# Small moves in a gated mix of an S4D convolution and segmented attention: prologue order, who issues the reciprocals' transfers, and when the first row maxima are taken

## The chip, the cores and the metric

The kernel runs on one core of a Trainium2 chip. Times are device microseconds of one launch. A core has a matrix engine (PE, with its weight loads shown as PEld), a vector engine (DVE), a scalar engine (ACT), GpSimd (POOL) and SyncE (SP). SP, ACT and POOL can issue DMA transfers; each of these engines works through its own instructions in order. Three timed runs of the kernel before gave 769.55, 772.67 and 773.4 us, so the time before is their median, 772.67 us.

## The reference, cut to what matters

Two branches read the same input `x` (2048 positions, 448 channels) and are mixed by a gate.

```python
g = sigmoid((x * gate_w).sum(-1))
# branch a: S4D. K is a 2048-long filter per channel, from 256 complex modes
dt = exp(log_dt); A = -exp(log_A_real) + 1j * A_imag
C = (C_real + 1j * C_imag) * dt
K = 2 * real(einsum("dn,dnl->dl", C, exp(A * dt * l)))
a = causal_convolution(x, K) + x * D_skip
# branch b: 16 heads of 28, 4 segments of 512 positions
q, k, v = x @ wq, x @ wk, x @ wv
for s in range(4):
    a_dot = softmax(q_s k_s^T * scale + causal_mask) @ v_s
    a_mem = phi(q_s) M / (phi(q_s) z + 1e-6)
    o_s = sigmoid(beta) * a_mem + (1 - sigmoid(beta)) * a_dot
    M += phi(k_s)^T v_s; z += sum(phi(k_s))
b = concat(o) @ wo
out = g * a + (1 - g) * b
```

## The kernel before, in words

The program has three parts that follow each other.

**The prologue** (`prepare_params`, the first 60 us). The parameters of 448 x 256 modes lie as 112 partitions x 1024. DVE and ACT turn them into decays, phases and amplitudes. The amplitude and the angle of C come from `mx` and `mn`, the larger and the smaller of |C_real| and |C_imag|: `f` is the reciprocal of `mx` (`v.reciprocal(f, mx)`), then `f * mn`, whose arctangent `g` ACT takes; cosine and sine of `g` come later. Phases go out in two quantities: `a` (a rounded number of turns from A_imag) and `d` (the angle of C, rounded). Each is split into three bf16 parts by `parts`: ACT copies the value to a bf16 tile `sp`, the value less that copy is formed for the next part, and the tile is sent to DRAM (`SP<-sp`, issued by ACT). Six such transfers leave; `load_phase` then reads them back as `lh<-SP` on SP's queue, and the main loop of the next part needs them. Decays take the same road through `SD`, with POOL subtracting and issuing. The amplitudes are transposed on PE and copied to `cab`. An identity matrix with its sign turned, `nid`, lets PE form a low part as x minus its rounded value (`rest` in `project`, with the results `wvl`). The weights `wv` arrive in four loads `winv` on SP's queue. ACT needs the tables of different functions in turn, each change being an `ACT_TABLE_LOAD`.

**The first part** (60 to 420 us). A loop over 56 half blocks makes the filter: PE forms exponents and turns (`ps_arg`), ACT takes exp and sine, DVE multiplies (`X`, `Y`), PE sums (`ps_k`). The projections to q, k and v, and the first step of the transform of x, are fed between by a planner with costs (`Feed`, `RATES`, `ITEMS`).

**The second part** (420 us to the end, `second_half`). After a transform of the filter in eight rounds come 16 units `i`, one for each segment and group of four heads, each of six rounds `r`. In a round PE makes scores for the unit's weights (`weigh`: `ps_w`, exponentiated by ACT to `PT`, masked by POOL's affine select) and scores for the row maxima of the unit after next (`maxima`: `ps_mx`, reduced by DVE to `mx`). When a unit's maxima are done, PE transposes them (`ps_m<-ident,mx`), ACT copies them with turned sign to `mn`, and POOL sends `mn` into a spare row of the unit's q tile (`qu<-mn`); the unit's weights cannot start before that lands. `values` multiplies `PT` with v (`ps_pv`). The convolution's frequency steps (`convolve`: `ps_c`, products `pr` on DVE, copies `ks` and `bs` on ACT) and the ends of segments (`seg_end`) are put between. `turn_over` issues matmuls on a constant tile `wz` whose result nobody reads. The order on each engine is the order in which the code calls its helpers, which pin it: line 1538 of the profile is the helper for matmuls, 1541 for transposes, 1492 the one that orders ACT and DVE, 1554 the one for SP's DMAs.

At the end of a segment, `norm` and `recall` each need reciprocals: the denominators are spread over 128 partitions (`dn`, `dm`), `inverse` takes the reciprocal on DVE, splits it into two parts `rs`, and sends each part to rows of `r8` (`r<-rs` in the profile, line 1138, issued by ACT; six pairs in all). PE spreads these rows over the heads (`ps_m<-r,sel`), and DVE scales by the result. The PSUM tiles for these spread rows, and for the outputs `po`, alternate between the tags `m` and `c` where both are free.

Of the kernel before, what the change touches and what calls it, by code (L numbers as in the profile page):

```python
# [16 lines left out]
AF = mybir.ActivationFunctionType  # L17
# [6 lines left out]
D = 448  # L24
# [156 lines left out]
def prepare_params(nc, k, pool, early, gp):  # L181
# [69 lines left out]
    k.chained = last["v"].ins  # L251
    ts(dtp, dt, 1.0 / TWO_PI, None, ALU.mult)
    ts(dt2, dt, 2.0, None, ALU.mult)
    v.reciprocal(f, mx)
    yield 4
    nc.gpsimd.tensor_tensor(la, la, wide(dt), ALU.mult)
    for _ in parts(k.SD, la, nc.gpsimd.tensor_tensor, k.pdma):
        pass
    tt(mn, b, c, ALU.min)
    tt(f, f, mn, ALU.mult)  # L260
    act(g, f, AF.Arctan)
    yield 4
# [10 lines left out]
    ts(ai, a, 32.0, None, ALU.mult)  # L273
    ts(e, ai, MAG, None, ALU.add)
    stt(ai, e, MAG, ai, ALU.subtract, ALU.subtract)
    tt(cr, d, cr, ALU.subtract)
    nc.scalar.activation(cr, cr, AF.Abs)
    stt(ai, a, 0.5, ai, ALU.mult, ALU.add)
    ts(ci, ci, 0.0, -2.0, ALU.is_lt, ALU.mult)
    ts(ci, ci, 1.0, None, ALU.add)  # L280
    yield 2
# [2 lines left out]
    tt(ci, ci, ai, ALU.add)  # L284
    ts(e, ci, MAG, None, ALU.add)
    stt(d, e, MAG, ci, ALU.subtract, ALU.subtract)
    pa, pd = parts(k.SP[:, :, 0], a, tt, k.adma), parts(k.SP[:, :, 1], d, tt, k.adma)
    for s in range(3):
        for x in (pa, pd):
            next(x)  # L290
        yield 1
    act(c, g, AF.Sin, bias=math.pi / 2, scale=-1.0)
    act(b, g, AF.Sin)
    yield "phases"
# [6 lines left out]
    for nt in range(2):  # L301
        pt = k.ps("m")
        for j in range(4):
            k.tr(
                pt[:, 112 * j : 112 * j + 112], mx[:, j, 128 * nt : 128 * nt + 128], k.ident[:112, :112]
            )
        v.tensor_copy(
            k.cab[:, nt].rearrange("n (p j) -> n j p", j=4), pt[:, :D].rearrange("n (j p) -> n j p", j=4)
        )


# [412 lines left out]
def project(nc, k, pp, early, filling):  # L724
# [12 lines left out]

    nid = early.tile([112, 112], F32R, name="nid")
    with k.issue_after(k.chained):
        v.tensor_scalar(nid, k.ident[:112, :112], -1.0, None, ALU.mult)  # L740

    def rest(lo, x, hi):

# [240 lines left out]
def attend(nc, k, ap):  # L984
# [142 lines left out]
    def inverse(x, rows, dst):  # L1127


        rc = ap.tile([128, 64], F32, tag="rc", name="rc", bufs=2)  # L1130
        rs = ap.tile([128, 2, 64], F32R, tag="rs", name="rs", bufs=2)
        v.reciprocal(rc, x)
        v.tensor_copy(rs[:, 0], rc)
        v.tensor_tensor(rs[:, 1], rc, rs[:, 0], ALU.subtract)
        yield
        for b in range(2):
            o = rows + 4 * b
            k.pin(k.adma(
                dst[o : o + 4].rearrange("o h (i f) -> o (h i) f", f=64).bitcast(F32),
                rs[:, b].bitcast(F32),  # L1140
            ))
# [4 lines left out]
    def recall(s):  # L1146

        dn = ap.tile([128, 64], F32, tag="dm", name="dm", bufs=1)
        k.ldma(dn, k.DM[s - 1].rearrange("j h (i f) -> (j h i) f", f=64))
        yield  # L1150
        am[s] = ap.tile([128, 4, SEG], F32, tag="am", name="am", bufs=1)
        k.ldma(am[s], k.AM[:, :, s - 1].rearrange("h p q -> p h q"))
        yield
        v.tensor_scalar(dn, dn, 1e-6, None, ALU.add)
        yield from inverse(dn, 32, r8)
        yield
        for hg in range(4):
            pb = k.ps("c")[:, 0] if s == 3 and hg % 2 else k.ps("m")
            k.mm(pb, k.sel[32:40], r8[32:40, hg], start=True, stop=True)
            v.scalar_tensor_tensor(am[s][:, hg], am[s][:, hg], k.gh[:, hg : hg + 1], pb, ALU.mult, ALU.mult)  # L1160
            yield

    def norm(s):

        pvs = pvss[s]
        dn = ap.tile([128, 64], F32, tag="dn", name="dn", bufs=1)
        k.pin(k.pdma(
            dn,
            pvs.rearrange("(j e) h q -> e j (h q)", e=32)[28].rearrange("j (i f) -> j i f", f=64),
        ))  # L1170
        yield
        yield from inverse(dn, 0, r8)
        yield
        for hg in range(4):
            o = pvs[:, hg]
            pb = k.ps("c")[:, 0] if s == 2 and hg % 2 else k.ps("m")
            k.mm(pb, k.sel[0:8], r8[0:8, hg], start=True, stop=True)
            v.scalar_tensor_tensor(o, o, k.omg[:, hg : hg + 1], pb, ALU.mult, ALU.mult)
            if s > 0:
                v.tensor_tensor(o, o, am[s][:, hg], ALU.add)  # L1180
            yield
# [41 lines left out]
    def seg_end(s):  # L1223
# [26 lines left out]
        for t in range(4):  # L1250
            if t < 3:
                next(memory)
            po = k.ps("c")[:, 0] if s == 2 and t % 2 else k.ps("m")
            out_mm(s, t, po[:, :D], range(2))
            half.append(s)
            yield "po"
            half.pop()
            out_mm(s, t, po[:, :D], range(2, 4))
            store(s, t, po[:, :D], xts[t])
            yield "po"  # L1260
# [52 lines left out]
def second_half(nc, k, ap, tp, fp, fin):  # L1313
# [82 lines left out]
    for i in range(16):  # L1396
# [5 lines left out]
        for r in range(6):  # L1402
# [4 lines left out]
            if r < 2:  # L1407
# [2 lines left out]
                if i + r == 0:  # L1410
                    turn_over(4)
                peak(behind)
            if i == 0 and r in (0, 2):
                turn_over(4 - r)
                peak(behind)
            k.spread = r in (1, 2)
# [16 lines left out]
            if (i, r) in DIVIDE:  # L1433
                if k.half:
                    step(ends[0])
                k.divide(DIVIDE[i, r])
            if 1 <= i <= 12:
                x = next(cv, "rest")
                if x == "more":
                    step(cv)  # L1440
                busy = busy or x != "rest"
# [334 lines left out]
```

## Time and the profile before

| what | value |
|---|---|
| timed runs | 769.55, 772.67, 773.4 us |
| the profiled execution, its own time | 768.64 us |
| its span | 766.6 us (2.0 us lie around it) |
| PE busy | 677.8 us (88%) |
| DVE busy | 560.4 us (73%) |
| ACT busy | 502.8 us (66%) |
| POOL busy | 160.0 us (21%) |
| mean granted PE clock | 0.982 |

The span runs from the first instruction to the last. A line of the timeline gives start, length, engine, source line, operation, output and input tile, shapes, a count, and in brackets the time that the engine sat idle just before and what released it. A line of the windows view gives for a stretch of time its length and the busy time of PE, PEld, DVE, ACT and POOL (with counts), then the granted PE clock, the mean share of the DMA engines and GB/s. The chain of waits follows the work that ended last back to its start.

### The profile page before, as it was taken

The numbers are of one execution on the slowest core, as the hardware profiler recorded it, in microseconds if no ns is written. First come the engines' busy times: TensorE is split into PE (matmuls) and PEld (weight loads), VectorE is DVE, ScalarE is ACT, GpSimd is POOL, SyncE is SP. The second block draws the span as 40 slices with busy tenths as digits, with TensorE's granted clock in tenths as the row PEclk, the third lists the DMA queues.
The fourth block names the chain that finished last, engine by engine and source line by source line (L and its number), as shares of the span: only waits on it lengthen the run. The fifth ranks groups of instructions, "written<-read, shape, count | busy, mean of one in ns | idle before, by whom it ended". The sixth has DMA issues, their size and how long they took to land.

```text
span 766.6 us, 19838 instructions
## 1 busy us (share of the span) xinstructions
PE 677.8 (88%) x8295; PEld 369.8 (48%) x8295; DVE 560.4 (73%) x758; ACT 502.8 (66%) x621; POOL 160.0 (21%) x196
## 2 busy tenths in 40 slices
PE   1685998899898999989999998989999889988997
PEld 1362565566554764556665443433343334434433
DVE  7989778878899878899788334656664775576585
ACT  4777679888999889989887533565634463452220
POOL 5404301110111011100120002242411241133110
PEclk9998999999999999999999999999899999999999
DMA  9427774333574335641455878999866977548597
GB/s 235 141 67 236 229 247 127 107 110 111 177 230 136 111 102 183 207 161 49 152 194 200 322 260 304 279 357 360 270 233 200 354 231 255 212 129 322 140 285 224
DMA packets 91490, 158.01 MB, mean 206 GB/s; under 512 B 22090, under 2 KB 59458, under 8 KB 91402
## 3 DMA queue, kind: packets, MB, share of 16 engines
q1 hardware_dynamic: 85722, 153.55, 60.8%
q10 hardware_dynamic: 4656, 2.23, 1.2%
q8 instruction: 65, 1.06, 0.6%
q0 software_dynamic: 1024, 0.98, 0.4%
q14 instruction: 23, 0.19, 0.1%
HBM read 88.51 MB, written 60.24 MB: 194 GB/s over the span
## 4 chain that ended last, share of the span: by engine, by line
PE 50%; ACT 18%; DVE 13%; DMA 11%; issue 5%; SPq 2%; POOL 1%; ACTq 0%; DVEq 0%; POOLq 0%
PE ps_m L1538 19%; PE ps_c L1538 9%; ACT cs L1492 5%; PE ps_w L1538 5%; PE ps_arg L1538 4%; PE ps_pv L1538 4%; PE ps_mx L1538 4%; PE ps_k L1538 3%; ACT EY L1492 2%; DVE mx L1492 2%; DVE pr L1492 2%; DMA WD<-wsp 2%; DMA rest<-TB 1%; DVE pvs L1492 1%; DMA w<-WD 1%
## 5 line engine op out<-in xcount | busy, mean ns | idle before, releaser
L1492 DVE TENSOR_REDUCE mx<-ps_mx 128x2 f32<-128x1024 f32 (+3 forms) x128 | 102.5, 822 | 92.9 <-PE ps_mx L1538 83.2
L1492 ACT ACTIVATE PT<-ps_w 128x1024 f32<-128x1024 f32 (+1 forms) x96 | 84.5, 880 | 112.7 <-PE ps_w L1538 104.9
L366 POOL TENSOR_TENSOR EX<-EX,cab 128x1024 f32<-128x1024 f32 x28 | 53.5, 1913 | 288.6 <-ACT EX L1492 266.3
L1492 ACT ACTIVATE cs<-ps_arg 128x1024 f32<-128x1024 f32 x97 | 94.5, 1023 | 3.5 <-DVE Y L414 2.4
L1538 PE MATMUL ps_w<-qu,ku 32*128 32x512 f32 (+3 forms) x768 | 88.1, 345 | 6.9 <-ACT PT L1492 5.1
L1538 PE MATMUL ps_m<-xh,w 112*128 112x512 f32 x256 | 91.6, 410 | 1.0 <-DMA w<-WD 1.0
L1538 PEld LDWEIGHTS ps_w<-qu,ku 32*128 32x128 f32 x768 | 58.1, 187 | 70.3 <-ACT PT L1492 33.2
L1099 POOL TENSOR_SCALAR_AFFINE_SELECT PT<-PT 128x256 f32<-128x256 f32 (+1 forms) x96 | 47.4, 494 | 211.4 <-ACT PT L1492 210.7
L409 DVE TENSOR_TENSOR X<-EX,cs 128x1024 f32<-128x1024 f32 x56 | 70.3, 1255 | 12.8 <-ACT cs L1492 11.8
L1538 PE MATMUL ps_k<-Y,X 128*32 128x64 f32 x3584 | 63.8, 225 | 14.1 <-DVE Y L414 14.1
L1538 PEld LDWEIGHTS ps_k<-Y,X 128*32 128x32 f32 x3584 | 54.5, 113 | 40.2 <-DVE Y L414 22.9
L413 DVE TENSOR_TENSOR Y<-EY,cs 128x1024 f32<-128x1024 f32 x56 | 69.2, 1236 | 0.0
L1492 ACT ACTIVATE cs<-cs 128x1024 f32<-128x1024 f32 x56 | 59.2, 1057 | 1.3
L1538 PEld LDWEIGHTS ps_m<-xh,w 112*128 112x128 f32 x256 | 48.1, 188 | 21.1 <-issue 8.4
L1492 ACT ACTIVATE EY<-ps_arg 128x1024 f32<-128x1024 f32 x52 | 51.1, 1036 | 4.3 <-PE ps_arg L1538 4.1
L1538 PE MATMUL ps_arg<-ct,lh 64*128 64x512 bf16 x224 | 45.9, 385 | 7.0 <-ACT EY L1492 4.7
L1538 PE MATMUL ps_m<-xl,w 112*128 112x512 f32 x128 | 50.3, 393 | 0.0
L1538 PEld LDWEIGHTS <-lh 64*128 64x128 bf16 x392 | 20.0, 94 | 59.3 <-issue 46.9
L1538 PE MATMUL ps_pv<-PT,V 128*32 128x128 f32 (+3 forms) x512 | 44.2, 443 | 0.0
L1538 PE MATMUL ps_mx<-ku,qu 32*128 32x512 f32 (+3 forms) x256 | 43.4, 371 | 0.0
L415 DVE SCALAR_TENSOR_TENSOR Y<-EY,cs 128x512 f32<-128x512 f32 x56 | 40.0, 715 | 3.8 <-ACT cs L1492 2.5
L1538 PE MATMUL ps_arg<-ce,lh 64*128 64x512 bf16 x168 | 33.1, 399 | 10.8 <-ACT EY L1492 6.6
(224 smaller groups left out, 1296.5 us busy)
## 6 DMA issues: line engine op xcount, KB each, us to landing
w<-WD SPq DMA_DIRECT2D x32, 448.0 KB
qu<-QD SPq DMA_DIRECT2D x16, 512.0 KB
ku<-KD SPq DMA_DIRECT2D x16, 512.0 KB
GU<-gs SPq DMA_DIRECT2D x32, 224.0 KB
GK<-gs SPq DMA_DIRECT2D x8, 896.0 KB
gk<-GK SPq DMA_DIRECT2D x16, 448.0 KB
gu<-GU SPq DMA_DIRECT2D x16, 448.0 KB
ks<-ks SPq DMA_DIRECT2D x32, 224.0 KB
```

The source lines that it names most:

```text
L366: nc.gpsimd.tensor_tensor(o, o, cab, ALU.mult)
L409: v.tensor_tensor(X, ex, t[:, :, 0], ALU.mult)
L413: v.tensor_tensor(Y[:, :, :, :32], lo, y[:, :, :, ::-1], ALU.mult)
L415: v.scalar_tensor_tensor(Y[:, 1, :, 32:], ey[:, :, 32:], -1.0, y[:, 1], ALU.mult, ALU.mult)
L1099: nc.gpsimd.affine_select(sl, sl, pat, ALU.is_ge, 0.0, base=0, channel_multiplier=-1)
L1492: x = op(*args, **kw)
L1538: tc.keep_in_program_order(nc.tensor.matmul(*args, **kw))
```

## The change

In the prologue, `mn` is formed ahead of the reciprocal; `nid` and the two copies to `cab` go from DVE to ACT; the last step of `ai` moves ahead of the step on `cr`; the first part of `a` is split and sent sooner, so that the three rounds of (a, d) become one round of `a` alone, two rounds with both and one with `d` alone. In the second part, the twelve transfers `r<-rs` are issued by POOL in place of ACT; the third piece of unit 1's maxima in unit 0 comes in round 1 instead of round 2, with three fillers ahead of it instead of two; four fillers are added in unit 12, round 5; and the alternation between `c` and `m` starts with `c` in three places.

```diff
@@ prepare_params
+    tt(mn, b, c, ALU.min)
     v.reciprocal(f, mx)
     yield 4
     nc.gpsimd.tensor_tensor(la, la, wide(dt), ALU.mult)
     for _ in parts(k.SD, la, nc.gpsimd.tensor_tensor, k.pdma):
         pass
-    tt(mn, b, c, ALU.min)
     tt(f, f, mn, ALU.mult)
...
     stt(ai, e, MAG, ai, ALU.subtract, ALU.subtract)
+    stt(ai, a, 0.5, ai, ALU.mult, ALU.add)
     tt(cr, d, cr, ALU.subtract)
     nc.scalar.activation(cr, cr, AF.Abs)
-    stt(ai, a, 0.5, ai, ALU.mult, ALU.add)
+    pa = parts(k.SP[:, :, 0], a, tt, k.adma)
+    next(pa)
     ts(ci, ci, 0.0, -2.0, ALU.is_lt, ALU.mult)
...
-    pa, pd = parts(k.SP[:, :, 0], a, tt, k.adma), parts(k.SP[:, :, 1], d, tt, k.adma)
-    for s in range(3):
-        for x in (pa, pd):
-            next(x)
-        yield 1
+    pd = parts(k.SP[:, :, 1], d, tt, k.adma)
+    next(pa)
+    next(pd)
+    yield 1
+    next(pa)
+    next(pd)
+    yield 1
+    next(pd)
+    yield 1
...
-        v.tensor_copy(
-            k.cab[:, nt].rearrange("n (p j) -> n j p", j=4), pt[:, :D].rearrange("n (j p) -> n j p", j=4)
+        act(
+            k.cab[:, nt].rearrange("n (p j) -> n j p", j=4), pt[:, :D].rearrange("n (j p) -> n j p", j=4), AF.Copy
         )
@@ project
-        v.tensor_scalar(nid, k.ident[:112, :112], -1.0, None, ALU.mult)
+        act(nid, k.ident[:112, :112], AF.Copy, scale=-1.0)
@@ inverse
-            k.pin(k.adma(
+            k.pin(k.pdma(
@@ recall
-            pb = k.ps("c")[:, 0] if s == 3 and hg % 2 else k.ps("m")
+            pb = k.ps("c")[:, 0] if s == 3 and hg % 2 == 0 else k.ps("m")
@@ norm
-            pb = k.ps("c")[:, 0] if s == 2 and hg % 2 else k.ps("m")
+            pb = k.ps("c")[:, 0] if s == 2 and hg % 2 == 0 else k.ps("m")
@@ seg_end
-            po = k.ps("c")[:, 0] if s == 2 and t % 2 else k.ps("m")
+            po = k.ps("c")[:, 0] if s == 2 and t % 2 == 0 else k.ps("m")
@@ second_half
-            if i == 0 and r in (0, 2):
+            if i == 0 and r < 2:
                 turn_over(4 - r)
                 peak(behind)
...
                 k.divide(DIVIDE[i, r])
+            if (i, r) == (12, 5):
+                turn_over(4)
```

The first place is ACT's order in the prologue, from the last copy of the low weights (`wvl`) to the parts of `d`. `EY` and `EX` are the first exponentials, `sp<-pin_a` and `sp<-pin_d` the bf16 copies of the phases, `pin_cr` the absolute value on which `d` depends. Before:

```order
L1513 ACTIVATE wvl<-ps_m 112x448
L277 ACTIVATE pin_cr<-pin_cr 112x1024
L1501 ACT_TABLE_LOAD
L1501 ACTIVATE EY<-ps_arg 128x1024 x2
L1501 ACTIVATE EX<-ps_arg 128x1024
L1501 ACTIVATE EY<-ps_arg 128x1024 x2
L1501 ACTIVATE EX<-ps_arg 128x1024
L1513 ACTIVATE sp<-pin_d 112x1024
L236 DMA SP<-sp 448x1x256
L1513 ACTIVATE sp<-pin_a 112x1024
```

And now:

```order
L1521 ACTIVATE wvl<-ps_m 112x448
L1509 ACT_TABLE_LOAD
L1509 ACTIVATE EY<-ps_arg 128x1024
L278 ACTIVATE pin_cr<-pin_cr 112x1024
L1509 ACTIVATE EY<-ps_arg 128x1024
L1521 ACTIVATE sp<-pin_a 112x1024
L1509 ACTIVATE EX<-ps_arg 128x1024
L236 DMA SP<-sp 448x1x256
L1509 ACTIVATE EY<-ps_arg 128x1024 x2
L1509 ACTIVATE EX<-ps_arg 128x1024
L1521 ACTIVATE sp<-pin_d 112x1024
```

The copy of `a`'s second part and its DMA moved up between the exponentials, and `pin_cr` moved down behind the table load and the first exponential.

The second place is POOL at the start of the units: the sends of `mn` for units 0 and 1, between the masks of unit 0. Before:

```order
L990 MEMSET wo 128x1792
L1062 DMA qu<-mn 4x4x128
L1099 AFFINE_SELECT PT<-PT 128x2x128 x3
L1062 DMA qu<-mn 4x4x128
L1099 AFFINE_SELECT PT<-PT 128x2x128
L1099 AFFINE_SELECT PT<-PT 128x2x256 x2
```

And now:

```order
L996 MEMSET wo 128x1792
L1068 DMA qu<-mn 4x4x128
L1105 AFFINE_SELECT PT<-PT 128x2x128 x2
L1068 DMA qu<-mn 4x4x128
L1105 AFFINE_SELECT PT<-PT 128x2x128 x2
L1105 AFFINE_SELECT PT<-PT 128x2x256 x2
```

Unit 1's send now stands behind two masks in place of three, so one round sooner.

The third place is the third pair of reciprocal transfers, at the end of segment 1 (unit 8). Before, on ACT, they stand between two exponentials of `PT`:

```order
L1492 ACTIVATE ks<-ps_c 128x896
L1492 ACTIVATE PT<-ps_w 128x2x256
L1492 ACTIVATE PT<-ps_w 128x2x512
L1138 DMA r_5457<-rs 4x32x64 x2
L1492 ACTIVATE PT<-ps_w 128x2x512
L1492 ACTIVATE mn<-ps_m 16x128
L1492 ACTIVATE xt<-xt,gt 128x448 x2
```

Now they stand on POOL, between masks, behind the send that gathers the denominators (`dn<-pvs`):

```order
L1173 DMA dn<-pvs 128x1x64
L1105 AFFINE_SELECT PT<-PT 128x2x128
L1105 AFFINE_SELECT PT<-PT 128x2x256 x2
L1144 DMA r_5457<-rs 4x32x64 x2
L1105 AFFINE_SELECT PT<-PT 128x2x128 x2
L1068 DMA qu<-mn 4x4x128
L1200 TENSOR_TENSOR xt<-xt,dbc 128x448 x2
```

ACT's exponential no longer stands behind the pair; two of POOL's masks and the next unit's `qu<-mn` do.

## The prediction

> **What bounds the kernel now.** I read the page's chain of waits first, then the windows of the second part, then the idle times before PE's instructions.
>
> ```profile
> span 766.6 us, 19838 instructions
> PE 50%; ACT 18%; DVE 13%; DMA 11%; issue 5%; SPq 2%; POOL 1%; ACTq 0%; DVEq 0%; POOLq 0%
> 500.00:640.00 140.00, 129.24 (x1572) 55.51 (x1565) 88.12 (x117) 72.28 (x99) 42.83 (x70) 0.98 0.84 288
> 640.00:767.00 127.00, 114.23 (x944) 49.58 (x942) 81.08 (x113) 39.27 (x53) 24.20 (x42) 0.98 0.67 216
> ```
>
> In the second part PE is busy 129.24 of 140 us, that is 92%; POOL is busy 31% there. So a stop of PE there is lost time, and POOL has room. What one stop costs is more than its length, as the windows of 3.41 us along the granted clock show:
>
> ```profile
> 472.69:476.10 3.41, 1.79 (x25) 0.71 (x24) 1.14 (x2) 0.90 (x2) 0.64 (x1) 1.00 0.86 292
> 476.10:479.52 3.42, 3.42 (x28) 1.20 (x24) 0.40 (x1) 1.33 (x2) 0.41 (x1) 0.50 0.11 40
> 540.95:544.37 3.42, 2.39 (x37) 1.45 (x37) 3.42 (x6) 2.81 (x5) 3.42 (x5) 1.00 0.94 324
> 544.37:547.78 3.41, 3.41 (x33) 1.49 (x29) 0.92 (x3) 1.48 (x2) 0.65 (x3) 0.50 0.28 69
> 547.78:551.19 3.41, 3.41 (x33) 1.08 (x25) 1.69 (x3) 1.46 (x2) 0.99 (x2) 0.50 0.71 260
> 612.63:616.05 3.42, 2.03 (x36) 1.12 (x39) 1.26 (x2) 2.13 (x4) 0.92 (x2) 1.00 0.96 362
> 677.49:680.90 3.41, 1.95 (x25) 0.85 (x20) 3.41 (x6) 1.19 (x2) 1.27 (x2) 1.00 0.39 144
> 680.90:684.31 3.41, 3.32 (x22) 0.92 (x24) 2.17 (x6) 0.00 (x0) 0.00 (x0) 0.50 0.00 0
> ```
>
> Behind a window with PE busy 1.79, 2.39 or 1.95 us the clock is 0.50 for one or two windows, in which PE is busy throughout and the others wait; behind one with 2.03 it stays at 1.00, so the limit is not sharp. A window at half clock does 1.71 us of PE's work, which at full clock and 92% takes 1.85 us: an estimate of 1.56 us lost for each, and four of them stand in the second part.
>
> The Trainium skill (TensorE: Matmul & The Clock Gate, "What's actually happening") has the clock halve after an idle window of about 3.4 us; the length agrees with these windows, the condition does not, since PE was busy 1.79 to 2.39 us in those ahead of the drops.
>
> **The prologue: the front hides behind a load.**
>
> ```profile
> 19.03 2.51 DVE L214 TENSOR_TENSOR pin_mn<-pin_b,pin_c 112x1024 f32<-112x1024 f32 x1
> 23.25 1.21 DVE L214 TENSOR_TENSOR pin_f<-pin_f,pin_mn 112x1024 f32<-112x1024 f32 x1
> 25.91 1.06 ACT L214 ACTIVATE pin_g<-pin_f 112x1024 f32<-112x1024 f32 x1
> 20.62 2.69 SPq L1624 DMA_DIRECT2D gb<-in_B_beta  x4
> 23.40 0.37 SPq L756 DMA_DIRECT2D winv<-in_B_wv  x1
> 27.60 0.58 ACT L1513 ACTIVATE wvh<-winv 112x448 fp32r<-112x448 f32 x1 [0.64 <-DMA winv<-in_B_wv]
> ```
>
> With `nid` gone and `mn` ahead, DVE has `f` up to 3 us sooner (`mn` costs 2.51 here, 1.21 like the next product where it runs alone). Yet ACT's arctangent stands behind other work, and all that follows it behind `wvh` at 27.60, which waits for the fourth `winv`. SP issued that at 23.40, having been busy with `gb` until 23.31. A sooner DVE brings it at most 0.1 us. I take 0. `nid` on ACT lies in idle time ahead of the first weights.
>
> **The prologue: the tail.**
>
> ```profile
> 37.20 0.54 ACT L1513 ACTIVATE wvl<-ps_m 112x448 fp32r<-112x448 f32 x1 [1.02 <-PE ps_m L1538]
> 37.64 1.05 ACT L277 ACTIVATE pin_cr<-pin_cr 112x1024 f32<-112x1024 f32 x1
> 39.99 1.94 ACT L1501 ACTIVATE EY<-ps_arg 128x1024 f32<-128x1024 f32 x2
> 45.43 1.10 ACT L1513 ACTIVATE sp<-pin_d 112x1024 bf16<-112x1024 f32 x1
> 52.39 0.70 ACTq L236 DMA_DIRECT2D SP<-sp  x1
> 57.36 1.28 ACT L1494 ACT_TABLE_LOAD   x1
> 57.85 1.75 DVE L214 COPY cab<-ps_m 128x448 f32<-128x448 f32 x2 [0.32 <-PE ps_m L1541]
> 60.69 1.02 ACT L1494 ACTIVATE cs<-ps_arg 128x1024 f32<-128x1024 f32 x1 [2.04 <-DVE cs L386]
> ```
>
> ACT leaves 37.7 as before. Until the first copy of `d` it does the same table load, `pin_cr` and six exponentials, and in addition one copy of `a` (about 1.05): that copy starts near 46.5, not 45.43. From there one copy and one DMA fewer stand in the tail, but its steps follow each other: copy (1.1), subtract (1.2), copy, subtract, copy is 5.7 us, and `a`'s third copy with a DMA issue of 0.6 stands between the first two. The last `SP<-sp` leaves near 52.6, against 52.39: +0.2. Bounds: +1.1, when the whole extra copy stays, and -1.6, one copy and its issue saved. PE's value matmuls also begin an exponential later, which meets the same end. `cab` on ACT (two of about 0.6) comes ahead of its table load and fills idle time that was 2.04, while DVE is free sooner: +0.1, between -0.4 and +0.6. **The prologue: +0.3.**
>
> **The first maxima.**
>
> ```profile
> 464.73 1.02 ACT L1492 ACTIVATE PT<-ps_w 128x1024 f32<-128x1024 f32 x1 [3.80 <-PE ps_w L1538]
> 466.93 1.02 ACT L1492 ACTIVATE PT<-ps_w 128x1024 f32<-128x1024 f32 x1 [1.17 <-PE ps_w L1538]
> 468.69 0.61 POOL L1062 DMA_DIRECT2D qu<-mn  x1 [0.27 <-POOL PT L1099]
> 472.26 0.61 PE L1538 MATMUL ps_pv<-wz 128*128 128x512 bf16 x2
> 474.49 0.50 PE L1538 MATMUL ps_w<-qu,ku 32*128 32x512 f32 x2 [1.62 <-DMA qu<-mn]
> ```
>
> PE waits 1.62 us for unit 1's `mn`. A round here is 2.2 us (464.73 to 466.93), and the send moves up by one: that covers the wait. Late next is ACT's last exponential of unit 0, which frees the scores' tile: I leave 0.4 for it, an estimate, so 1.2 is won. Net one filler more is issued, some 0.2 us by the row of two. And the clock window at 476.10 should stay whole: -1.56. **-2.6**, between 0 and -3.2.
>
> **The reciprocals' transfers.**
>
> ```profile
> 536.03 7.01 DMA r<-rs
> 543.18 0.47 PE L1538 MATMUL ps_m<-r,sel 8*128 8x512 f32 x1 [0.70 <-DMA r<-rs]
> DMA to landing us min/median/max: 3.5/6.1/6.5
> 611.84 2.04 ACTq L1138 DMA_DIRECT2D r<-rs  x2
> 613.92 1.02 ACT L1492 ACTIVATE PT<-ps_w 128x1024 f32<-128x1024 f32 x1 [4.43 <-DVE mx L1492]
> 615.00 0.45 PE L1538 MATMUL ps_w<-qu,ku 32*128 32x384 f32 x2 [1.39 <-ACT PT L1492]
> 686.72 1.23 ACT L1492 ACTIVATE xt<-xt,gt 128x448 f32<-128x448 f32 x2 [0.41 <-DMA r<-rs]
> ```
>
> From ACT the first pair's second part lands 7.01 us after its issue, and PE waits 0.70 us. POOL has no row of its own for this transfer; the nearest is `dn<-pvs`, of the same 32 KB in pieces of the same 256 bytes, which lands after 3.5 to 6.5 us, 6.1 in the middle. Issued at 536.03 it lands at 542.1, ahead of PE's 542.48. So the wait goes (-0.7) and the two windows at half clock behind it (-3.1): **-3.8**, between 0 and -4.
>
> In the third pair ACT's exponential at 613.92 starts only when the two issues end (611.84 and 2.04 make 613.88), and PE waits 1.39 us for it. On POOL that block is gone: **-1.4**, between -0.5 and -1.8. In the fifth ACT waits 0.41 for the issue, and PE behind it: **-0.4**. At the other three no PE wait ends on ACT or on the transfer: 0. What now queues behind a waiting pair are POOL's masks and the next `qu<-mn`; the masks serve `values` a unit later, and POOL idles more than half the time, which hides two issues of 0.6.
>
> **The fillers of unit 12 and the tags.**
>
> ```profile
> 680.99 3.26 PE L1538 MATMUL ps_c<-pr,cb 64*64 64x448 f32 x16 [1.50 <-DVE pr L1492]
> 710.76 0.28 PE L1541 MATMUL ps_m<-ident,mx 128*16 128x128 f32 x1 [0.83 <-DVE tb L1492]
> ```
>
> Four fillers (about 1.0 us) go where PE waits 1.50 for `pr`: they cost nothing while that wait stands, and up to 1.0 if it is gone. They lift the window at 677.49 from 1.95 to some 2.8 us, above every row that fell: **-1.6**, between +1.0 and -1.6. With the tags exchanged the transpose at 710.76 no longer shares its tile with the output just before it, whose sum `tb` it awaits: **-0.8**; other pairs meet instead, so +0.8 is the other bound.
>
> **Sum**: 0.3 - 2.6 - 3.8 - 1.4 - 0.4 - 1.6 - 0.8 = -10.3. On the profiled execution's own 768.64 us (766.6 and 2.0 around) that is 758.3. The runs' median, 772.67, lies 4.0 above that execution; on it the sum gives 762.4, and I predict **762**.
>
> **The rivals.**
>
> The half-clock windows are not bought. For: three windows with 1.79, 1.95 and 2.03 busy had two fates, and one with 2.39 fell; a stop elsewhere may fall instead. Against: each drop here follows a window with a stop that goes. Then the waits alone are won: -1.0 - 0.7 - 1.4 - 0.4 - 0.8 + 0.3 = -4.0, or 768.7. The skill's clock page points the same way, by its idle window: stops of 1 to 2 us would not decide the clock.
>
> Other waits take over everywhere: the DMA engines' share is 0.84 from 500 to 640 us and 0.94 in the window at 540.95, so a PE that is sooner may meet loads that are not, and 5 us won early could be handed back. Against: beside `qu<-mn` and `r<-rs`, PE's idle rows longer than 0.3 us there name ACT and DVE, and no load of q, k or the convolution. About -0.5: 772.
>
> The front's 3 us come through after all, since SP and PE end almost together ahead of `winv`: -3 more, 759.4. The rows of `gb` speak against it.
>
> **Slower**: POOL's sends land late. They stand behind masks that wait for ACT, and a landing that is 3 us later than ACT's 7.0 makes PE wait 3 us more at each of the three norms: +9, with a half-clock window at each +4.7, against -6.5 from the rest: +7.2, or 780. It decides from a landing of about 9.2 us on (three times 2.2 eats 6.5). Against: no `dn<-pvs` took over 6.5. The skill (SBUF — State Buffer, "A bandwidth-pool intuition that's wrong") speaks for it: GpSimd cannot write its descriptors while DVE holds the port they share, and 620 ns become 3100. By that the landing of 6.1 would be an estimated 8.6 and the sum near -2. The rows here show no such lateness.
>
> **How the numbers follow.** Forecast 0.52 (756 to 766), the front comes through 0.06, clock not bought 0.22, taken over 0.12, slower 0.08. The range must leave out no more than two in ten: 756 to 770 leaves out the slower case, half of the taken-over one and a small tail below. A measurement tells this kernel from no change at about 0.5%, 3.9 us, so faster means below 768.8: 0.52 and 0.06, with 0.13 of the clock case, which lies on that line: 0.71. Within: 0.21. Slower: 0.08.
>
> **What would show it.** Right: the first `cs` of the loop near 61 us; no `qu<-mn` wait ahead of unit 1; no `r<-rs` wait; ACT's exponential in unit 8 directly behind its scores; clock 1.00 after unit 0, in segment 0's end and in unit 12. Wrong: a first `cs` that moves by more than 1 us, new drops of the clock in the second part, `r<-rs` from POOL landing after more than 7 us, or PE waiting for loads.

## The result, and the profile after

| kernel | timed runs, median | ratio to the kernel before, 95% interval |
|---|---|---|
| before, beside the changed one | 771.13 us (4 runs) | |
| changed | 761.99 us (760.22 to 762.35, 4 runs) | 0.9875 [0.9839, 0.9910] |
| changed, a second time | 761.63 us (759.63 to 763.95, 10 runs) | 0.9913 [0.9882, 0.9945] |

The change makes the kernel 0.9 to 1.3% faster; 762 us was forecast. Some executions run 5 to 40 us longer than the others of their kernel, the longest of them at a lower mean clock; they are left out of every ratio and mean here.

The page and the windows view of the changed kernel answer to the first rows of the prediction: PE's share of the chain rose from 50 to 55%, the transfers' fell from 11 to 5%, and between 500 and 640 us the granted clock is 1.00 (0.98 before).

```profile
span 760.4 us, 19830 instructions
PE 55%; ACT 18%; DVE 13%; issue 5%; DMA 5%; SPq 2%; POOL 1%; DVEq 0%; ACTq 0%; POOLq 0%
500.00:640.00 140.00, 130.22 (x1596) 56.52 (x1596) 92.45 (x124) 73.59 (x100) 49.37 (x80) 1.00 0.86 291
640.00:761.00 121.00, 110.25 (x895) 47.90 (x896) 75.77 (x103) 37.45 (x50) 25.52 (x44) 0.97 0.68 220
```

To see where the time went, the program is cut at eight instructions that both kernels have: A the first `cs` of the loop, B the end of the filter, C the first product with v (in unit 1), D a product with `pr` in unit 4, E the first output product of segment 0, F a product with `pr` in unit 10, G the first output product of segment 2, H the first `bt`. In the timeline of the kernel before, B to H are these rows (A, at 60.69, stands in the prediction):

```profile
421.27 1.77 PE L1538 MATMUL ps_w<-kb,s1k 32*128 32x448 f32 x8 [0.30 <-DVE kb L436]
475.38 1.28 PE L1538 MATMUL ps_pv<-PT,V 128*32 128x512 f32 x8
531.12 0.98 PE L1538 MATMUL ps_c<-pr,cb 64*64 64x448 f32 x8 [0.47 <-DVE pr L1492]
556.00 1.40 PE L1538 MATMUL ps_m<-wo,pvs 128*128 128x448 f32 x3
627.51 1.74 PE L1538 MATMUL ps_c<-pr,cb 64*64 64x448 f32 x16 [1.19 <-DVE pr L1492]
696.72 1.77 PE L1538 MATMUL ps_m<-wo,pvs 128*128 128x448 f32 x4 [0.89 <-DVE pvs L1492]
720.48 1.72 PE L1538 MATMUL ps_c<-bt,fc 128*64 128x448 f32 x8
```

And A to H in the timeline of the changed one:

```profile
62.35 1.02 ACT L1502 ACTIVATE cs<-ps_arg 128x1024 f32<-128x1024 f32 x1
422.65 1.77 PE L1546 MATMUL ps_w<-kb,s1k 32*128 32x448 f32 x8 [0.30 <-DVE kb L442]
475.50 1.06 PE L1546 MATMUL ps_pv<-PT,V 128*32 128x512 f32 x8
529.67 0.98 PE L1546 MATMUL ps_c<-pr,cb 64*64 64x448 f32 x8 [0.46 <-DVE pr L1500]
551.37 1.77 PE L1546 MATMUL ps_m<-wo,pvs 128*128 128x448 f32 x4
621.41 1.74 PE L1546 MATMUL ps_c<-pr,cb 64*64 64x448 f32 x16 [1.19 <-DVE pr L1500]
688.56 1.86 PE L1546 MATMUL ps_c<-wo,pvs 128*128 128x448 f32 x2 [0.88 <-DVE pvs L1500]
713.27 2.51 PE L1546 MATMUL ps_c<-bt,fc 128*64 128x448 f32 x6
```

The differences of such starts, in us, for these two and for the experiments below, as far as their profiles are used (the last column runs to the end of the span):

| kernel | to A | A-B | B-C | C-D | D-E | E-F | F-G | G-H | H-end |
|---|---|---|---|---|---|---|---|---|---|
| before | 60.69 | 360.58 | 54.11 | 55.74 | 24.88 | 71.51 | 69.21 | 23.76 | 46.12 |
| changed | 62.35 | 360.30 | 52.85 | 54.17 | 21.70 | 70.04 | 67.15 | 24.71 | 47.13 |
| after_again | 62.67 | 357.39 | 52.92 | 54.18 | 21.68 | 70.05 | 67.14 | 24.31 | 47.56 |
| maxima_old | 60.75 | 359.50 | 53.66 | 54.15 | 21.81 | 70.01 | 67.14 | 24.75 | 48.73 |
| prologue_old | 60.65 | 361.49 | 52.85 | 54.16 | 22.57 | 70.05 | 67.13 | 25.26 | 47.04 |
| unit12_old | 61.39 | 360.52 | 52.88 | 54.18 | 21.71 | 70.07 | 68.78 | 26.63 | 47.34 |
| recip_pool_alone | 60.72 | 360.48 | 54.18 | 54.16 | 21.70 | 70.10 | 69.35 | 26.39 | 46.42 |
| fillers_alone | 61.01 | 357.65 | 53.72 | 54.19 | 22.61 | 71.47 | 67.60 | 26.41 | 59.34 |
| fillers_two | 60.30 | 361.28 | 54.02 | 54.16 | 23.74 | 73.81 | 69.10 | 23.75 | 48.24 |
| fillers_three | 58.90 | 360.89 | 53.72 | 54.17 | 29.99 | 72.47 | 67.58 | 25.58 | 48.60 |
| cab_dve | 61.54 | 360.57 | 52.87 | 54.18 | 21.70 | 70.04 | 67.15 | 24.33 | 47.62 |
| fill_13 | 59.86 | 360.69 | 52.88 | 54.17 | 21.70 | 70.06 | 67.14 | 22.75 | 45.95 |
| fill_first | 60.79 | 357.52 | 53.32 | 54.21 | 22.02 | 73.75 | 67.13 | 23.15 | 47.91 |

Where nothing differs, a stage repeats within 0.1 us (54.15 to 54.21 in C-D, without the drop that stood there before); so what differs can be read. Between the two kernels five stages of the second part win 1.26, 1.57, 3.18, 1.47 and 2.06 us, and the last two give back 0.95 and 1.01. These last hold something new: a drop, that is a window at half clock, at two places that had none. Stretches of 3.41 us in the changed kernel, first at the three places whose drops went, then at the two where drops came (all but the first two lie on the edges of the clock's own windows):

```profile
476.10:479.50 3.40, 3.40 (x45) 1.18 (x41) 1.76 (x2) 2.49 (x4) 0.41 (x1) 1.00 0.84 217
544.40:547.80 3.40, 3.01 (x49) 1.18 (x41) 1.75 (x4) 1.46 (x3) 1.27 (x2) 1.00 0.92 299
674.82:678.23 3.41, 3.33 (x40) 1.20 (x40) 3.04 (x7) 1.49 (x2) 1.15 (x2) 1.00 0.02 5
685.06:688.47 3.41, 1.51 (x18) 0.69 (x17) 3.38 (x6) 0.66 (x2) 1.47 (x3) 1.00 1.03 418
688.47:691.88 3.41, 3.32 (x8) 1.21 (x10) 2.67 (x5) 0.00 (x0) 0.00 (x0) 0.50 1.03 409
708.95:712.36 3.41, 3.20 (x32) 1.78 (x23) 2.67 (x4) 2.08 (x3) 0.80 (x2) 1.00 0.41 128
712.36:715.78 3.42, 3.42 (x15) 1.45 (x14) 0.08 (x1) 0.60 (x1) 0.64 (x1) 0.50 1.04 253
```

The two stops between 685 and 688.5 us (0.96 us for `mx`, 0.88 for `pvs`) stood in the kernel before too, 1.00 and 0.89 us that ended at 694.68 and 696.72. There a window ended at 694.55, just ahead of the first stop's end, and shared the two out:

```profile
691.14:694.55 3.41, 2.53 (x32) 1.41 (x32) 3.28 (x5) 1.42 (x2) 2.91 (x4) 1.00 1.02 414
694.55:697.97 3.42, 2.27 (x19) 1.19 (x18) 3.35 (x7) 0.60 (x1) 0.64 (x1) 1.00 1.03 407
```

Now one window holds both, PE works 1.51 us in it, and the next runs at half clock. At the second place, 708.95, there is hardly a stop: PE works 3.20 us of 3.41. What is special about that window is said in the last section.

### The profile page after: what moved, and what is told of

Same layout as the page of the kernel before. It is cut to its first block, busy times and chain, and to the rows that moved or that the text cites. A ratio compares the mean times of both kernels' runs of the same rounds, so it can differ in the third digit from the quotient of the medians.

```text
span 760.4 us, 19830 instructions
## 1 busy us (share of the span) xinstructions
PE 673.1 (89%) x8284; PEld 368.6 (48%) x8300; DVE 556.8 (73%) x755; ACT 504.7 (66%) x624; POOL 167.2 (22%) x208
## 3 DMA queue, kind: packets, MB, share of 16 engines
q10 hardware_dynamic: 3072, 1.84, 0.9%
q0 software_dynamic: 1600, 1.39, 0.8%
q8 instruction: 65, 1.06, 0.6%
## 4 chain that ended last, share of the span: by engine, by line
PE 55%; ACT 18%; DVE 13%; issue 5%; DMA 5%; SPq 2%; POOL 1%; DVEq 0%; ACTq 0%; POOLq 0%
PE ps_m L1546 20%; PE ps_c L1546 10%; PE ps_w L1546 6%; ACT cs L1500 6%; PE ps_pv L1546 5%; PE ps_mx L1546 4%; PE ps_arg L1546 4%; PE ps_k L1546 4%; ACT EY L1500 2%; DVE pr L1500 2%; DVE mx L1500 2%; DMA WD<-wsp 2%; DVE pvs L1500 2%; DMA ce<-in_c_ce 1%; ACT L1500 1%
```

## The experiments

Twelve runs were made in three groups, each group on one chip and beside its own runs of the kernel before. Differences are between means of the runs, with standard errors. A drop is a stretch of one or more windows at half clock.

### Without the reciprocals' transfers on POOL (recip_on_act)

```diff
-            k.pin(k.pdma(
+            k.pin(k.adma(
```

> The changed kernel itself, timed in the same call as the three below so that they can be compared with it. Expected 0.9875 of the kernel before, so near 762 us where before takes 771.5. In its profile the half-clock windows are what matters: if they hang on stops of PE that are part of the program, the two of the second part come again at the end of unit 12 and in unit 14 (near 688 and 712 us); if they hang on how the free-running windows of 3.41 us happen to lie, at least one of them is gone or stands elsewhere.

> The changed kernel with the transfers of the reciprocals issued by ACT again. Theory (the sum of the prediction): -3.8 - 1.4 - 0.4 = -5.6 comes back, so 5.6 us above the changed kernel, with the wait for the first pair, the block of 1.4 us in unit 8 and one or two half-clock windows behind the first pair in the profile. Rival (clock windows were not bought by this): only the waits, 0.7 + 1.4 + 0.4 = 2.5 us come back. A second rival (POOL's later sends cost something elsewhere): below 1 us.

The changed kernel came to 761.84 ± 0.41 us, this one to 766.54 ± 0.61 (ratio 0.9983 [0.9951, 1.0015]): 4.7 ± 0.7 us come back, near the 5.6 of the theory and over the 2.5 of the waits alone. Of this kernel only the times are used, so where they come back isn't shown. In the changed kernel's second profile both drops of the second part stand at the same program places (686.6 and 710.5 us), and both of the first part are gone: so in these two executions the former repeat and the latter don't.

### The reciprocals' transfers on POOL alone (recip_pool_alone)

```diff
@@ the kernel before, inverse
-            k.pin(k.adma(
+            k.pin(k.pdma(
```

> The kernel before with the transfers of the reciprocals issued by POOL, and nothing else changed. Theory: 5.6 us faster than the kernel before, about 766, no PE wait for r in segment 0's end and clock 1.00 there. Rival without the clock: 2.5 us faster. Rival (it helps only together with the rest, since the end is reached through other waits): under 1 us.

764.80 ± 0.73 against 769.81 ± 0.80 us, 0.9933 [0.9901, 0.9965]: 5.0 ± 1.1 us faster. The stages D-E and E-F are those of the changed kernel to 0.06 us. F-G is not: without the fillers of unit 12 two windows at half clock stand there.

This kernel takes the first maxima as before, and PE waits for unit 1's send as before (1.50 us, where it was 1.62). Yet no drop follows:

```profile
474.48 0.50 PE L1538 MATMUL ps_w<-qu,ku 32*128 32x512 f32 x2 [1.50 <-DMA qu<-mn]
472.48:475.89 3.41, 1.91 (x26) 0.72 (x25) 1.24 (x2) 1.00 (x2) 0.64 (x1) 1.00 0.79 255
475.89:479.30 3.41, 3.41 (x45) 1.11 (x41) 1.83 (x2) 2.49 (x4) 0.41 (x1) 1.00 0.59 193
```

The window holds 1.91 us of PE's work, against 1.79 in the kernel before, and C-D is 54.16 without the sooner maxima. So the drop behind unit 0 is not tied to the wait alone.

### Without the sooner maxima (maxima_old)

```diff
-            if i == 0 and r < 2:
+            if i == 0 and r in (0, 2):
```

> The changed kernel with the third piece of unit 1's maxima in round 2 again. Theory: the wait for the send of unit 1 returns (1.0 net) with its half-clock window (1.56), so 2.6 us above the changed kernel. Rival without the clock: 1.0 us. If other waits had taken over: 0.

764.84 ± 0.59, so 3.0 ± 0.7 us slower than the changed kernel. But its profile splits this otherwise than the theory: B-C costs 0.81 more (53.66 against 52.85), and no drop follows in C-D, though PE waits 1.17 us for the send again: the window with that wait, at 471.58, holds 2.25 us of work. The rest lies in the finish, H-end, 1.6 more than in the changed kernel, where PE now waits for a load:

```profile
734.96 1.73 PE L1546 MATMUL ps_c<-bt,fc 128*64 128x448 f32 x8 [1.53 <-DMA bt<-BB]
738.10 1.72 PE L1546 MATMUL ps_mx<-bt,fc 128*64 128x448 f32 x8 [0.86 <-DVE pvs L1500]
```

The helper for SP's transfers holds each of them behind a marked instruction (`issue_after`) but doesn't fix their order among themselves; the scheduler put a load of `bt` two transfers later here. So the 3.0 is no clean price of the maxima.

### Without the change to the prologue (prologue_old)

All six edits in `prepare_params` and `project` are undone: `tt(mn, b, c, ALU.min)` behind the reciprocal again, the last step of `ai` behind `cr`, three rounds of both phases, `nid` and `cab` on DVE.

> The changed kernel with the whole prologue of before (minimum behind the reciprocal, first parts of both phases together, the sign-turned identity and the two copies on DVE). In the profile after, the first sine and cosine of the loop stand at 62.35 against 60.69, 1.7 us later; of that about 1.0 was there already when the fourth load of weights came in, and 0.6 arose at the two copies on ACT and the last parts. Theory A (the change in the prologue costs what that profile shows): 1.7 us faster than the changed kernel, first cs near 60.7. Theory B (only the copies and the tail cost; the 1.0 at the loads was one execution's luck): 0.6 faster, with the fourth weights at 27.6 to 28.6 in both kernels from one execution to the next. Rival C (the sooner front gains): the changed kernel is faster, by up to 3 us.

761.57 ± 0.66 against 761.84 ± 0.41: no difference that can be seen. Over all profiles the fourth `wvh` comes anywhere from 26.46 to 28.62 us, with either prologue, so the first 1.0 us of the later `cs` was that execution's luck (28.62 against 27.60). What follows it can be compared: from that `wvh` to the first `cs` the six kernels with the old prologue take 32.44 to 33.39 us, mean 33.0, four with the new one and the copies on ACT 33.45 to 34.73, mean 34.1. The profiles speak for theory B, with a tail that costs about 1.1; the timing (0.3 ± 0.8 us) speaks against the 1.7 of theory A and can't tell B from 0.

### Only the two copies back on DVE (cab_dve)

```diff
-        act(
+        v.tensor_copy(
             k.cab[:, nt]...
```

> The changed kernel with only the two copies of the amplitudes back on DVE. On ACT they took 1.77 us between the last copies and the table load that the first cosine needs; on DVE 1.75 us beside that load. Theory: the table load starts 0.5 to 1.3 us sooner and the first cs with it, so 0.5 to 1.3 us faster than the changed kernel. Rival (the first cs waits for DVE's preparation of its argument anyway, 2.04 us of idle time in the kernel before): 0 or up to 0.4 slower.

761.68 ± 0.40, beside 769.81 for the kernel before; against the changed kernel's 761.84 of another group this tells nothing below 1 us. In three profiles with the copies on DVE, `wvh` to `cs` takes 33.90, 33.15 and 33.28 us, mean 33.4: some 0.6 less than with the copies on ACT. The timeline of ACT in the changed kernel shows why:

```profile
59.27 1.77 ACT L214 ACTIVATE cab<-ps_m 128x448 f32<-128x448 f32 x2 [0.51 <-PE ps_m L1549]
61.06 1.28 ACT L1502 ACT_TABLE_LOAD   x1
```

The table load stands directly behind the copies, and the first `cs` (62.35) directly behind the load; in the kernel before, with the copies on DVE, the load was over by 58.64 (57.36 and 1.28) and the idle time of 2.04 us hid it.

### The fillers without the waits (fillers_alone, fillers_two, fillers_three)

```diff
@@ the kernel before, second_half (r is the round, i the unit)
+            if (i, r) == (0, 5):
+                turn_over(5)
+            if (i, r) == (12, 5):
+                turn_over(4)
@@ norm
+            if s + hg == 0:
+                k.fill(3)
             k.mm(pb, k.sel[0:8], r8[0:8, hg], start=True, stop=True)
```

> The kernel before with unread matmuls put where PE waited ahead of the three drops of the clock in the second part, and no wait removed: five at the end of unit 0, three ahead of the first spread of reciprocals, four in unit 12 (these four are also in the change). At 0.25 us each they fill 1.2 of 1.62, 0.7 of 0.70 and 1.0 of 1.50 us. Theory (the stop ahead of a window decides the drop, 1.56 us each): four windows at half clock go, so up to 6.2 us faster than the kernel before, about 765.3 where before takes 771.5, with a granted clock of 1.00 behind unit 0, in the end of segment 0 and in unit 12, and the landing of the transfers unchanged. Rival (the drops don't hang on these stops): 0, between 1 slower and 1 faster, with the drops at the same places.

A ratio of 1.0146 [1.0066, 1.0227], from three runs only (776.03 to 786.15 us): slower, against theory and rival. Yet no drop stands at the three places; the windows of its profile that answer to 476, 544 and 680 us of the kernel before:

```profile
473.40:476.81 3.41, 3.41 (x45) 1.16 (x41) 1.33 (x2) 2.17 (x4) 0.81 (x2) 1.00 0.49 161
541.67:545.08 3.41, 2.87 (x45) 1.15 (x47) 2.26 (x4) 1.99 (x4) 1.27 (x2) 1.00 0.88 247
674.80:678.21 3.41, 3.41 (x49) 1.29 (x43) 2.64 (x5) 1.90 (x2) 0.26 (x1) 1.00 0.13 44
```

All run at 1.00. C-D is 54.19 in place of 55.74: one drop costs 1.55 us. How much of this is the fillers' doing differs by place. At the first, the drop is missing in recip_pool_alone and maxima_old too, without fillers. At the second only the kernel before shows the transfers on ACT without fillers, and with the same fillers four windows fell there in fillers_three (below). In unit 12 it is theirs: all four profiles without fillers there (the kernel before, recip_pool_alone, fillers_two, unit12_old) have a drop between 673 and 681 us, and none of the nine others that are compared here. What was lost stands in H-end, 59.34 in place of 46.12, with a wait that no other kernel has, and windows at half clock ahead of it (three from 712.32) and around its end (two from 746.46):

```profile
749.86 3.26 PE L1545 MATMUL ps_mx<-bt,fc 128*64 128x448 f32 x8 [7.76 <-DMA bt<-BB]
```

SP's order there had come out anew. From the first pair of `rest<-TB` behind the long run of loads on, the kernel before issues (x2 is two of a kind):

```
bt; rest<-TB x2; bt; YD x2; out x2; YD x2; out x2; YD x2; out; rest<-TB x2; out; ...
```

and fillers_alone:

```
rest<-TB x2; bt; YD x2; out x2; YD x2; out; rest<-TB x2; out; bt; ...
```

The last load `bt` comes ten transfers later, behind stores and two loads of `rest`.

Two more runs part the fillers from that order, one without the four in unit 12, one with three of them (there both loads follow the first pair of `rest<-TB` directly):

> The run with fillers and no wait removed once more, without the four in unit 12: five at the end of unit 0 and three ahead of the first spread of reciprocals. SP's order in the finish, which had come out otherwise there (one load of bt behind five more transfers), stands as in the kernel before but for two stores of the output beside each other. Theory (a stop decides the drop): the windows at half clock behind unit 0 (one) and in segment 0's end (two) go, 3 x 1.56 = 4.7 us faster than the kernel before, if the later drops do not become more; both places at clock 1.00 in the profile, and no wait for bt over 1 us. Rival (the drops don't hang on the stops, or fillers cost as such): 0, or slower by up to 10 as in the first such run, with the drops in place.

> All three groups of fillers on the kernel before, as in the first such run but three in place of four in unit 12, which gives SP another order in the finish: the last load of bt is issued two transfers later than in the kernel before, not behind the five more. Theory (the loss of that first run, 10 us and more, was SP's order and not the fillers): no wait of PE for bt over 2 us, and 3 to 6 us faster than the kernel before. Rival (fillers as such slow the finish or the chip): 5 to 15 us slower again, with lower clocks.

They came to 769.94 ± 1.14 and 771.76 ± 1.24 beside 769.66 ± 0.63 us: the loss of 10 us is gone with the order (PE waits 0.95 and 1.21 us for `bt`), so it was SP's order and not the fillers: fillers_three has all of them but one. The expected gain isn't there either. In fillers_two C-D and D-E win 1.6 and 1.1, H-end loses 2.1 (part of it the wait for `bt`), and E-F gives 2.3 back, where the kernel before had stayed at full clock:

```profile
608.90:612.30 3.40, 1.30 (x14) 0.22 (x10) 2.32 (x3) 1.09 (x3) 0.00 (x0) 1.00 1.03 402
612.30:615.70 3.40, 3.40 (x44) 2.33 (x48) 1.29 (x2) 2.27 (x5) 3.26 (x5) 0.50 0.56 160
615.70:619.10 3.40, 3.40 (x37) 1.78 (x39) 0.48 (x1) 2.58 (x4) 2.54 (x3) 0.50 0.00 0
```

Here one window holds both stops of that place (0.94 us for `pr`, 1.16 for ACT's exponential, the block that POOL takes away in the changed kernel); in the kernel before a boundary lay between them, at 612.63. In fillers_three the wait for `r` outgrew its fillers: the transfer from ACT took 9.25 us in the chain of waits, PE idled 2.14 us behind them, and four windows ran at half clock (D-E 29.99).

```profile
532.53 9.25 DMA r<-rs
541.91 0.76 PE L1545 MATMUL ps_m<-r,sel 8*128 8x512 f32 x1 [2.14 <-DMA r<-rs]
538.10:541.50 3.40, 1.62 (x26) 0.86 (x24) 2.25 (x4) 2.21 (x4) 3.40 (x5) 1.00 0.73 244
```

### Without the fillers of unit 12 and with the old tags (unit12_old)

```diff
-            if (i, r) == (12, 5):
-                turn_over(4)
@@ recall, norm, seg_end
-  ... % 2 == 0 else k.ps("m")
+  ... % 2 else k.ps("m")
```

> The changed kernel without the four fillers of unit 12 and with the tags c and m alternating as before. The sum of the prediction had -1.6 for the fillers and -0.8 for the tags, so theory: 2.4 us slower than the changed kernel, with a half-clock window behind the wait for pr in unit 12 (near 674 to 681 us) and the wait of 0.83 us of the transpose back. Rival (by the profiles of the changed kernel, two half-clock windows stand at the end of unit 12 and in unit 14 in any case, so that the drop was only moved): 0.8 slower by the tags alone. Third: 0, within 1 us.

764.30 ± 0.73, 5.4 us below the kernel before of its group (the changed kernel lies 6.9 below in its own): about 1.6 us slower, with a standard error of 1.2, which can't tell 2.4, 0.8 and 0 apart. There F-G is 1.63 longer, with the wait and the drop where theory put them, and the transpose's wait is back:

```profile
674.23 2.15 PE L1544 MATMUL ps_c<-pr,cb 64*64 64x448 f32 x12 [1.50 <-DVE pr L1498]
706.23 0.28 PE L1547 MATMUL ps_m<-ident,mx 128*16 128x128 f32 x1 [0.83 <-DVE tb L1498]
671.10:674.50 3.40, 1.74 (x23) 0.88 (x27) 3.40 (x5) 0.98 (x2) 1.28 (x2) 1.00 0.30 115
674.50:677.90 3.40, 3.40 (x30) 1.33 (x24) 1.81 (x5) 0.68 (x1) 1.41 (x2) 0.52 0.04 5
```

### Fillers at the new drops, and a faster kernel (fill_13, fill_first)

```diff
@@ cab_dve, second_half
-                turn_over(3 if i == 0 or 0 < r < 5 else 2)
+                turn_over(6 if (i, r) == (13, 4) else 3 if i == 0 or 0 < r < 5 else 2)
@@ seg_end
+            if s == 2 and t == 0:
+                k.fill(3)
             out_mm(s, t, po[:, :D], range(2))
```

> The kernel of the run before this one (copies back on DVE) with six more unread matmuls in unit 13: three in round 4 ahead of the scores, where PE waits 0.96 us for the maxima's tile, and three ahead of the first output product of segment 2, where it waits 0.88 us. Theory (drops hang on stops): the half-clock window near 688 us goes, 1.56 us faster, less up to 0.3 for fillers that overrun; the one near 712 us stays. Rival: no drop is bought, 0 to 0.7 slower, as the scores start 0.75 later behind the first three.

758.89 ± 0.46 against 761.68 ± 0.40 for cab_dve in the same group, 0.9854 [0.9813, 0.9894] of the kernel before: 2.8 ± 0.6 us faster, more than expected. Its second part has no drop at all until PE's work ends. The one at 712 us went too, which the fillers did not aim at: a window edge, at 706.39 us, now lies between the matmuls of that place (last section). So part of the 2.8 is luck of position. Against cab_dve, G-H falls from 24.33 to 22.75 and H-end from 47.62 to 45.95.

```diff
@@ fill_13, decays
+            if i == 0 and g in (3, 11):
+                k.turn_over(kps[g - 1][:, 6:8], 10)
             if i < 4:
                 exponents(*todo[i + 2])
```

> The fastest kernel so far (copies back on DVE, six unread matmuls in unit 13) with ten unread matmuls more at each of the two places in the first part where PE waits 1.7 to 1.8 us for ACT's EY and the clock falls to half behind a window with 1.6 to 1.7 us of PE work. Ten take about 1.3 us there, inside the wait. Theory (the window falls when PE works less than half of it): both windows keep clock 1.00, up to 2 x 1.56 = 3.1 us faster than that kernel, less up to 1.5 for SP's order in the finish, which moves a load of bt by two transfers; near 757 to 759. Rival (in the first part ACT and DVE are busy 3.4 of 3.4 us around these places, so PE's loss is hidden): 0, within 1 us, although the clock stays.

758.66 ± 0.60, ratio 0.9848 [0.9815, 0.9881]. Both drops of the first part are gone and A-B falls from 360.69 to 357.52, that is 3.2 us: so PE's loss there is not hidden, against the rival. That the fillers did it is not shown: after_again and fillers_alone have none there, wait 1.7 to 1.8 us at both places, and miss both drops too (A-B 357.39 and 357.65). Here the waits are down to 1.13 and 1.06 us, and no window at those places holds less than 2.29 us of work. The profile of fill_first also has a drop of two windows near 605 us and one at 711, where fill_13 had none; E-F pays 3.7 for the first. The time is the same as fill_13's. Either is the fastest kernel of this study, about 1.5% below the kernel before.

## Why the prediction was right, and where not

| step | forecast | between the two profiles |
|---|---|---|
| prologue (to A) | +0.3 | +1.66, of it 1.02 ahead of `wvh` |
| filter loop (A-B) | 0 | -0.28 |
| first maxima, the wait (B-C) | -1.0 | -1.26 |
| first maxima, the clock (C-D) | -1.56 | -1.57 |
| first pair of `r<-rs` (D-E) | -3.8 | -3.18 |
| third pair (E-F) | -1.4 | -1.47 |
| fifth pair and fillers of unit 12 (F-G) | -2.0 | -2.06 |
| tags (G-H) | -0.8 | +0.95 |
| finish (H-end) | 0 | +1.01 |
| sum | -10.3 | -6.2 |

**The median was met in part by luck.** The saving was forecast at 10.3 us; 9.1 came between the medians, 6.9 between the means of the repeat, 6.2 between the profiles. The base, 772.67, was high: the kernel before ran at 771.13 beside the changed one and at means of 768.8 to 769.8 in the three groups of runs above. A saving taken too large and a base taken too high cancelled to 762. On the profiled execution the sum gave 758.3 us; the changed kernel's profiled one took 762.1. On the median it gave 762.4, and 762.0 came. The executions of the kernel before scatter more (762 to 773 us in one group) than those of the changed one (759.6 to 764), and the one that was profiled lay 2.5 us below its median of the result, the changed one at it. Which windows fell in the timed runs no profile shows, so this part stays open.

**The waits and their clock** came out near the forecast between the two profiles, to 0.1 us in C-D, E-F and F-G. The undone parts confirm two of the terms. The reciprocals' move is worth 4.7 and 5.0 us, taken away and alone, where the waits alone make 2.5. In unit 12 the drop goes with the fillers in every profile, and without them F-G is 1.63 longer. The wait of 1.39 us behind ACT's exponential, the third pair's block, is gone from PE's rows. The clock term of the first maxima, -1.56, is luck of this pair of profiles: with a wait of 1.50 and 1.17 us for the same send two other profiles had no drop there (1.91 and 2.25 us of work in the window). **The mis-sized terms**: the tail of the prologue, forecast at +0.2 for the copies of the phases and +0.1 for `cab`, is about +0.5 and +0.6; the copies on ACT did not fill idle time, since the table load behind them had used that idle time already. The prediction's own mark for being wrong, a `cs` later by over 1 us, was met in the profile, but 1.0 of the 1.66 was luck. The front is 0, as forecast, behind the fourth `winv`.

**What failed** is the step from "each drop here follows a window with a stop that goes" to a saving that stays. Drops came at two places that the change leaves alone, at 688 us with two stops of 0.9 us, at 712 with hardly any, because the program had moved against the windows: the edge that parted the two stops before, at 694.55, is gone from between them. Two executions of the changed kernel show the same without any edit. Their stops in the first part agree to 0.02 us, but the windows around them held 1.60 and 1.69 us of PE's work in one, and fell, 1.91 and 2.01 in the other, and stood. Of four half-clock windows in the second part two are left. For this the rival "not bought" had 0.22, and its sentence "a stop elsewhere may fall instead" is what happened at 688 us. The tags did take away the transpose's 0.83 us; the two new drops hide it in G-H (fill_13, without a drop, stands at 22.75 against 23.76 before).

**The other rivals.** Loads took over nowhere in the changed kernel. POOL's sends did not land late enough to matter: an issue takes 687 to 713 ns, and the landing is 3.3 to 8.4 us, 4.8 in the middle, below the 9.2 from which the slower case would decide. The third pair took 7.4 and 8.4 us, over the 7 that the prediction had named as a sign of being wrong; PE waited 0.29 us for it, and 0.36 for the same pair from ACT in the kernel before. By the Trainium skill (SBUF — State Buffer, "A bandwidth-pool intuition that's wrong") a transfer of about 620 ns that GpSimd issues takes about 3100 beside a copy on DVE, an estimated 2.5 us more. The median here lies below the 6.1 that the sum assumed without this; whether the third pair owes its length to it no run shows.

```profile
L1144 POOL DMA_DIRECT2D r<-rs x12: 687/700/713, 533.2 to 697.1; - x12
DMA to landing us min/median/max: 3.3/4.8/8.4
```

It isn't always in time: in prologue_old the first pair's second part took 7.40 us and PE waited 0.67, with D-E 0.9 longer and no drop.

## What to carry to other kernels

A stop of PE has two prices: its length, and 1.5 us for each window of the clock that it pulls below the mark, the work in a window under which the next one runs at half clock. The second depends on how stops fall into windows that are not tied to the program, so a saving in one place can be spent at the next stop: count all stops of more than half a microsecond, and give the clock term to the sum of them, not to each. One profile of the kernel before does not tell which drops it has in other executions. And look at the orders that a scheduler makes far from an edit: with four unread matmuls in unit 12 in place of three, one load on another queue came out ten transfers later, and the kernel some ten microseconds slower.

## What the runs showed of the hardware

**The clock falls when PE works less than about half of a window.** Between 80 and 420 us, in thirteen profiles (all but that of recip_on_act), every window of 3.41 us with PE busy 1.60 to 1.70 us was followed by one at 0.50; of four with 1.72 to 1.82 three were, and of those from 1.84 on none. Half of 3.41 is 1.71. The window with 1.72 that stood, in fillers_alone:

```profile
135.49:138.90 3.41, 1.72 (x70) 1.39 (x73) 3.41 (x7) 3.41 (x6) 0.00 (x0) 1.00 0.69 226
138.90:142.31 3.41, 3.40 (x42) 2.05 (x31) 3.15 (x6) 3.03 (x5) 1.92 (x1) 1.00 0.51 171
```

The Trainium skill (TensorE: Matmul & The Clock Gate, "What's actually happening") lets the clock halve after an idle window; here a window that is half busy is enough.

**In the second part windows fell with far more work**: 2.39 us in the kernel before at 540.95, 3.20 in the changed one at 708.95. Both hold matmuls of the reciprocals, with 8 rows of the array (`r,sel`), and so do all others that fell with more than 1.82, but one: 601.66 in fill_first fell with 2.02 us and no such matmul, where 2.03 stood at 612.63 in the kernel before and 1.91 at 472.48 in recip_pool_alone. At the place that stands near 712 us in the changed kernel four of them come within 2.5 us, in all of these kernels. In nine of the thirteen profiles one window holds all of them or nearly all (after_again is the loosest, with the first outside), and it falls with 3.19 to 3.25 us of work. In the other four an edge parts them two and two or three and one, and no window falls. That such matmuls count for nothing isn't enough: taken out, they leave 1.92 us at 540.95 before, which fell (2.39 less 0.47), and 1.78 at 694.55, which stood (2.27 less 0.49). Why the mark lies higher there stays open.

**A transfer of 32 KB from ACT's queue** took 7.01 us in the kernel before and 9.25 in fillers_three at the same place. Behind the same three fillers PE's wait for it was nothing in fillers_alone, 1.06 us in fillers_two and 2.14 in fillers_three.
